# Attention masks written straight from comparisons, their assembly moved to ACT and GpSimd, and the parameters loaded from ACT's queue

## The chip, the cores and the metric

The kernel runs on one core of a Trainium2 chip. The metric is the device time of one execution in microseconds (us), lower being better; the median of a few executions is compared. Engines are named as in the profile: PE (TensorE matmul), PEld (its weight loads), DVE (VectorE), ACT (ScalarE), POOL (GpSimd) and SP (SyncE, which issues most of the DMAs here).

## What is computed

Sliding-window attention with a few sink columns, then two feed-forward layers on the 1536 tokens that come out of it.

```
B, H, S, D = 2, 8, 768, 64;  n_sink, window = 4, 128        # both arrive at run time
scores = q @ k.T / sqrt(D)
keep   = (pos_k < n_sink) | ((0 <= pos_q - pos_k) & (pos_q - pos_k < window))
a      = softmax(where(keep, scores, -1e9));  x = a @ v     # 1536 x 512
x = (h * clip(h + 3, 0, 6) / 6) @ w_out    with h = x @ w_in      # d_ff = 2048
y = (h * sigmoid(1.702 * h)) @ w_out2      with h = x @ w_in2     # d_ff = 2048
```

## The kernel before

**Tiles.** The tokens are taken in 12 tiles of 128 queries, T0 to T11, six to each batch. A query tile sees its own keys, those of the tile ahead and the four sinks: 196 columns, put side by side in an order of their own. Three mask tiles of 128x196 hold 0 where a score is kept and LOW = -1e9/SCALE where it isn't: `masks[0]` for the first tile of a batch, `masks[1]` for the second, `masks[2]` for all others.

**One tile's softmax.** A tile is done in two halves ("duos") of two head pairs. For each duo PE makes the scores (L743, 48 matmuls in the trace). For each of its four heads DVE adds the mask and finds the row's extreme in one instruction (L758), ACT takes the exponential (L766), and DVE and ACT scale by the inverse sum (L774, L775, L783, L785). PE transposes (L794), ACT or DVE copies the result out of PSUM (`pts`), and PE multiplies by the values (L817, L825). ACT and DVE then write the tile's x as two parts, `xyh` and `xyl` (L844). The feed-forward layers follow with L509 (up) and L577 (down), every product in three parts; their weights arrive packed in `stage` and DVE and ACT unpack and split them (L421 to L449, L405, L490).

**Who sets the order.** The part ahead of the fast path (constants, parameters, masks) is ordered by the tile framework's scheduler. From `fast_path` on, `Plan` records every operation with the engines that could do it and a cost on each, and its `issue` places them one after another by those costs. The result is a fixed order for each engine, and each engine works through its own in order. PSUM has eight banks, given out by the plan.

**The start.** SP loads `par_i` (window and n_sink as integers, spread over 128 partitions), then the keys and queries of T0 and T1 (`wf` from `in_kq`; later kq tiles use the same names), their values (`vb`, `vc`), the first weights (`stage`), and so on; eight of SP's loads can be under way, and each further one waits until the load eight places ahead has landed. DVE makes `flag` out of `par_i` (all parameters within what the fast path can do), every engine loads that flag and branches on it (L187), and behind the branch stands the fast path. Between flag and branch DVE makes the window and sink numbers (`par`, L194 to L201) and the masks' parts: `cur` (this tile's own keys), `prv` (the keys of the tile ahead), `snk` and `nos` (the sinks kept, and the sinks dropped since the ordinary columns hold them). Each part is made as ones and zeros and then turned into 0 and LOW by a second instruction (L230). `masks[0]` is put together there (L233, L234). Behind the branch the plan's first operations make `prv1` (L677) and copy the twelve pieces of `masks[1]` and `masks[2]` (L403 on ACT, L405 on DVE and POOL), on whichever engine its costs favour.

Of the kernel before, what the change touches and what calls it, by code (L numbers as in the profile page):

```python
# [9 lines left out]
F32 = mybir.dt.float32  # L10
F32R = mybir.dt.float32r
BF16 = mybir.dt.bfloat16
I32 = mybir.dt.int32
AF = mybir.ActivationFunctionType
ALU = mybir.AluOpType
PSUM = bass.MemoryType.PSUM

P = 128
SINKS = 4
HALF = 64  # L20
BIG = 1.0e9
# [42 lines left out]
def tile_sink_window_attention_moe_moe2(  # L64
# [10 lines left out]
    nc = tc.nc  # L75
# [7 lines left out]
    SCALE = 1.0 / math.sqrt(D)  # L83
# [16 lines left out]


    par_i = const.tile([P, 4], I32, name="par_i")
    nc.sync.dma_start(out=par_i, in_=params.bitcast(I32).unsqueeze(0).to_broadcast([P, 4]))

    tok = [(b, i) for b in range(B) for i in range(NI)]
    NTILE = len(tok)
# [45 lines left out]
    for kind, n in FIRST:  # L152
# [30 lines left out]
        out=ge, in0=ge, in1=le, scale=1.0, scalar=0.0, op0=ALU.mult, op1=ALU.add, accum_out=okay  # L183
# [5 lines left out]
    lo_f = const.tile([P, 2], F32, name="lo_f")  # L189
    hi_f = const.tile([P, 2], F32, name="hi_f")  # L190
    neg = const.tile([P, 2], F32, name="neg")
    par = const.tile([P, 2], F32, name="par")
    par_v = par_i.rearrange("p (a b) -> p b a", b=2)
    nc.vector.tensor_copy(lo_f, par_v[:, 0, :])  # L194
    nc.vector.tensor_copy(hi_f, par_v[:, 1, :])

    nc.vector.tensor_scalar(
        out=neg, in0=lo_f, scalar1=0.0, scalar2=2.0**32, op0=ALU.is_lt, op1=ALU.mult
    )
    nc.vector.tensor_tensor(out=lo_f, in0=lo_f, in1=neg, op=ALU.add)  # L200
    nc.vector.scalar_tensor_tensor(  # L201
        out=par, in0=hi_f, scalar=2.0**32, in1=lo_f, op0=ALU.mult, op1=ALU.add
    )
    win = par[:, 0:1]
    nsk = par[:, 1:2]

# [4 lines left out]
    cur = const.tile([P, P], F32, name="cur")  # L211
    prv = const.tile([P, P], F32, name="prv")
    prv1 = const.tile([P, HALF], F32, name="prv1")
    snk = const.tile([P, HALF], F32, name="snk")
    nos = const.tile([P, HALF], F32, name="nos")
    LOW = -BIG / SCALE
    with tc.tile_pool(name="msk", bufs=1) as mp:
        grid = mp.tile([P, P], F32, name="grid")
        nc.gpsimd.iota(grid, pattern=[[-1, P]], base=0, channel_multiplier=1, allow_small_or_imprecise_dtypes=True)
        colc = mp.tile([P, HALF], F32, name="colc")  # L220
        nc.gpsimd.iota(colc, pattern=[[1, HALF]], base=0, channel_multiplier=0, allow_small_or_imprecise_dtypes=True)
        t0 = mp.tile([P, P], F32, name="t0")
        nc.gpsimd.memset(masks[0], LOW)
        nc.vector.tensor_scalar(out=t0, in0=grid, scalar1=0.0, scalar2=None, op0=ALU.is_ge)
        nc.vector.scalar_tensor_tensor(out=cur, in0=grid, scalar=win, in1=t0, op0=ALU.is_lt, op1=ALU.mult)
        nc.vector.tensor_scalar(out=snk, in0=colc, scalar1=nsk, scalar2=None, op0=ALU.is_lt)
        nc.vector.tensor_scalar(out=nos, in0=colc, scalar1=nsk, scalar2=None, op0=ALU.is_ge)
        nc.vector.tensor_scalar(out=prv, in0=grid, scalar1=float(P), scalar2=win, op0=ALU.add, op1=ALU.is_lt)
        for m in (cur, snk, prv, nos):
            nc.vector.tensor_scalar(  # L230
                out=m, in0=m, scalar1=1.0, scalar2=BIG / SCALE, op0=ALU.subtract, op1=ALU.mult
            )
        nc.vector.tensor_tensor(out=masks[0][:, HALF:P], in0=cur[:, :HALF], in1=snk, op=ALU.max)  # L233
        nc.vector.tensor_copy(masks[0][HALF:, P : P + HALF], cur[HALF:, HALF:])  # L234

# [163 lines left out]
    def copy(eng, out, in_):  # L401
        if eng is nc.scalar:
            eng.copy(out, in_)  # L403
        else:
            eng.tensor_copy(out, in_)  # L405
# [257 lines left out]
    def plan_attention(plan, pool, due):  # L663
# [5 lines left out]
        for t in pexps:  # L669
# [2 lines left out]
        top, low = slice(0, HALF), slice(HALF, P)  # L672
        both = slice(0, P)
        mask_b = [Buf() for _ in masks]
        prv_b = Buf()
        plan.op(
            [("DVE", 150)], lambda e: e.tensor_tensor(out=prv1, in0=prv[:, :HALF], in1=nos, op=ALU.min), None,  # L677
            writes=[prv_b],
        )
        parts = []  # L680
        for m, first in ((1, prv1), (2, prv)):
            parts += [
# [3 lines left out]
            ]  # L686
        for m, rows, a, n, src, x in parts:
            plan.op(
                [("ACT", 190), ("DVE", 110), ("POOL", 300)],
                lambda e, m=m, rows=rows, a=a, n=n, src=src, x=x: copy(  # L690
                    e, masks[m][rows, a : a + n], src[rows, x : x + n]
                ),
                None, reads=[prv_b], adds=[mask_b[m]],
            )

        kq_b = [Buf(kqt[T], at=landed.get(("kq", T))) for T in range(EARLY + KEPT)]
# [164 lines left out]
    def fast_path():  # L861
        with tc.manual_schedule(), tc.tile_pool(name="mlp", bufs=1) as pool, tc.tile_pool(
# [34 lines left out]
            def item_due(items):  # L897
# [4 lines left out]
                return due  # L902

            plan_attention(plan, ap, pair_due)
            plan_mlps(plan, BLOCKS, item_due)
            plan.issue()
# [160 lines left out]
```

## Time and profile before

| | |
|---|---|
| median of 3 executions | 634.97 us (634.57 to 635.03) |
| profiled execution, its own time | 633.52 us |
| span of the profile (first to last instruction) | 631.6 us |
| around the span | 1.9 us |
| busy: PE, PEld, DVE, ACT, POOL | 609.3, 495.3, 503.7, 260.3, 2.4 us |
| mean granted TensorE clock | 0.996 |

The page splits the span into 40 slices. PE is busy in nine tenths or more of nearly all of them; only the first two or three (some 16 us each) are not full. DMA is busy for all of the first 30 us and much less behind that. The profiled execution was 1.45 us shorter than the median of the three runs.

### The profile page before, as it was taken

How to read it: one execution, taken by the hardware profiler on the slowest of the kernel's cores; microseconds unless marked ns; L12 is line 12 of the kernel's file. 1: busy time of each engine (PE TensorE's matmuls, PEld its weight loads, DVE VectorE, ACT ScalarE, POOL GpSimd, SP SyncE). 2: the span in 40 equal slices, each digit the busy share in tenths (PEclk: the TensorE clock that was granted, in tenths of full speed). 3: DMA queues.
4: the chain of work that ended last, by engine and by line, in shares of the span. 5: the costliest groups of instructions: out<-in, count | busy, mean ns of one | idle time of the engine just before them, and what ended most of it. 6: DMA issues, size and time to landing. Idle time of an engine off the chain costs nothing.

```text
span 631.6 us, 10569 instructions
## 1 busy us (share of the span) xinstructions
PE 609.3 (96%) x4224; PEld 495.3 (78%) x4224; DVE 503.7 (80%) x1065; ACT 260.3 (41%) x548; POOL 2.4 (0%) x19
## 2 busy tenths in 40 slices
PE   4789999999999999999999999999999999999996
PEld 4667878887788888888888888888888888888885
DVE  7799999999857587699999999865766666766752
ACT  5887787766537221164443644212311112211111
POOL 1000000000000000000000000000000000000000
PEclk9999999999999999999999999999999999999999
DMA  8974442563400000003443323000100000100001
GB/s 265 377 220 139 158 160 85 172 205 134 155 1 2 1 1 0 1 7 137 153 171 116 129 90 133 1 0 1 67 2 0 1 1 1 67 0 1 0 1 71
DMA packets 11175, 50.91 MB, mean 81 GB/s; under 512 B 1456, under 2 KB 1456, under 8 KB 7024
## 3 DMA queue, kind: packets, MB, share of 16 engines
q1 hardware_dynamic: 11120, 50.18, 23.5%
q8 instruction: 35, 0.57, 0.4%
q14 instruction: 20, 0.16, 0.1%
HBM read 47.02 MB, written 3.15 MB: 79 GB/s over the span
## 4 chain that ended last, share of the span: by engine, by line
PE 79%; DVE 12%; ACT 4%; DMA 3%; issue 1%; SPq 0%; ACTq 0%; DVEq 0%
PE bank L509 37%; PE bank L577 37%; PE bank L743 2%; DMA stage<-in_w_dram 2%; DVE wf L449 2%; DVE pexp L758 2%; DVE wf L442 1%; ACT pexp L766 1%; PE bank L794 1%; DVE u L526 1%; DVE w1l L490 1%; DVE w0l L490 1%; PE bank L817 1%; DVE wf L434 1%; PE bank L825 1%
## 5 line engine op out<-in xcount | busy, mean ns | idle before, releaser
L509 PE MATMUL bank<-xyh,w0h 128*128 128x512 f32 x384 | 154.3, 402 | 1.4 <-ACT pts L403 0.7
L509 PE MATMUL bank<-xyl,w0h 128*128 128x512 f32 x384 | 151.1, 393 | 1.1 <-DVE xyl L844 1.1
L509 PE MATMUL bank<-xyh,w0l 128*128 128x512 f32 x384 | 151.6, 395 | 0.0
L535 ACT ACTIVATE u<-bank 128x512 f32<-128x512 f32 x48 | 28.8, 599 | 179.7 <-PE bank L509 179.6
L509 PEld LDWEIGHTS bank<-xyh,w0h 128*128 128x128 f32 x384 | 72.1, 188 | 18.4 <-ACT pts L403 0.9
L509 PEld LDWEIGHTS bank<-xyh,w0l 128*128 128x128 f32 x384 | 72.0, 187 | 18.0 <-DVE w0l L490 0.2
L509 PEld LDWEIGHTS bank<-xyl,w0h 128*128 128x128 f32 x384 | 72.1, 188 | 17.1 <-DVE xyl L844 1.4
L577 PE MATMUL bank<-gh,w1h 128*128 128x512 f32 x192 | 77.1, 402 | 0.0
L577 PE MATMUL bank<-w1h,gh 128*128 128x512 f32 x192 | 75.9, 395 | 0.0
L577 PE MATMUL bank<-gh,w1l 128*128 128x512 f32 x192 | 75.3, 392 | 0.6 <-DVE w1l L490 0.6
L577 PE MATMUL bank<-w1l,gh 128*128 128x512 f32 x192 | 75.4, 392 | 0.0
L577 PE MATMUL bank<-gl,w1h 128*128 128x512 f32 x192 | 75.1, 391 | 0.0
L577 PE MATMUL bank<-w1h,gl 128*128 128x512 f32 x192 | 75.1, 391 | 0.0
L405 DVE CAST w0h<-wf 128x512 fp32r<-128x512 f32 x81 | 34.4, 424 | 50.0 <-PE bank L509 49.9
L490 DVE TENSOR_TENSOR w0l<-wf,w0h 128x512 fp32r<-128x512 f32 x96 | 66.1, 689 | 4.8
L552 DVE TENSOR_TENSOR gl<-u,gh 128x512 fp32r<-128x512 f32 x96 | 66.1, 689 | 1.9
L490 DVE TENSOR_TENSOR w1l<-wf,w1h 128x512 fp32r<-128x512 f32 x96 | 66.1, 689 | 1.2
L521 ACT ACTIVATE u<-bank,three 128x512 f32<-128x512 f32 x48 | 33.0, 687 | 79.5 <-PE bank L509 79.2
L405 DVE CAST w1h<-wf 128x512 fp32r<-128x512 f32 x61 | 26.0, 427 | 35.9 <-PE bank L577 35.4
L766 ACT ACTIVATE pexp<-pexp,nb 128x196 f32<-128x196 f32 x96 | 43.2, 452 | 11.0 <-DVE nb L758 10.9
L577 PEld LDWEIGHTS bank<-w1h,gl 128*128 128x128 f32 x192 | 36.1, 188 | 8.6
L577 PEld LDWEIGHTS bank<-gh,w1l 128*128 128x128 f32 x192 | 36.1, 188 | 8.5 <-DVE w1l L490 0.9
(96 smaller groups left out, 819.0 us busy)
## 6 DMA issues: line engine op xcount, KB each, us to landing
stage<-in_w_dram SPq DMA_DIRECT2D x32, 1024.0 KB, 4.9
wf<-in_kq_dram SPq DMA_DIRECT2D x8, 520.0 KB, 11.1
vc<-in_vc_dram SPq DMA_DIRECT2D x12, 320.0 KB, 4.0
out_dram<-u SPq DMA_DIRECT2D x12, 256.0 KB, 2.1
vb<-in_v_dram SPq DMA_DIRECT2D x10, 256.0 KB, 6.1
kq<-in_kq_dram SPq DMA_DIRECT2D x4, 520.0 KB, 10.9
vb<-in_v_dram SPq DMA_DIRECT2D x4, 128.0 KB, 6.4
par_i<-in_params_dram SPq DMA_DIRECT2D x1, 2.0 KB, 2.8
```

Source lines behind the costliest of these rows:

```text
L405: eng.tensor_copy(out, in_)
L434: lambda e: e.tensor_scalar(out=w.tile, in0=w.tile, scalar1=3, scalar2=0x3FFFFFF8, op0=ALU.logical_shift_left, op1=ALU.bitwise_and,),
L449: lambda e: e.scalar_tensor_tensor(out=w.tile, in0=low, scalar=29, in1=w.tile, op0=ALU.logical_shift_right, op1=ALU.bitwise_or),
L490: lambda e: e.tensor_tensor(out=lo.tile, in0=src.tile.bitcast(F32)[:, cols], in1=hi.tile.bitcast(F32), op=ALU.subtract),
L509: e.matmul(h.tile[:, :n], w, x, start=(c == 0 and k == 0), stop=(c == NC - 1 and k == 2))
L521: lambda e: e.activation(u.tile[:, :n], h.tile[:, :n], AF.Relu, bias=three, scale=1.0),
L535: lambda e: e.activation(u.tile[:, :n], h.tile[:, :n], AF.Sigmoid, scale=1.702),
L552: lambda e: e.tensor_tensor(out=gl.tile[:, :n], in0=u.tile[:, :n], in1=gh.tile[:, :n].bitcast(F32), op=ALU.subtract),
L577: e.matmul(yb.tile, l, r, start=(begin and k == 0), stop=(end is not None and k == 2))
L743: e.matmul(sc[j].tile[c * HALF : (c + 1) * HALF, o : o + n], here[r, q0 + c * HALF : q0 + (c + 1) * HALF], src[r, at : at + n], start=True ...
L758: lambda e, j=j, n=n, cols=cols: e.tensor_tensor_reduce(out=pes[n].tile[:, :W], in0=sc[j].tile[:, cols], in1=masks[kind], scale=-SCALE, sc ...
L766: lambda e, n=n: e.activation(pes[n].tile[:, :W], pes[n].tile[:, :W], AF.Exp, bias=nbs[n].tile, scale=-1.0, accum_out=z.tile[:, n : n + 1],),
```

## The change

The parameters' load goes from SP's queue to ACT's. The parts of the masks come out of one comparison each: a comparison for "dropped" gives 1, and the second operation of the same instruction multiplies by LOW (`cur` still needs a second instruction). The distance to the tile ahead's keys has an iota of its own, `far`. `masks[0]`'s parts are written first, and `prv1` moves ahead of the branch. Behind the branch all six copies for `masks[1]` are given to ACT and all six for `masks[2]` to POOL; DVE has none.

```diff
-    nc.sync.dma_start(out=par_i, in_=params.bitcast(I32).unsqueeze(0).to_broadcast([P, 4]))
+    nc.scalar.dma_start(out=par_i, in_=params.bitcast(I32).unsqueeze(0).to_broadcast([P, 4]))
...
+        far = mp.tile([P, P], F32, name="far")
+        nc.gpsimd.iota(far, pattern=[[-1, P]], base=P, channel_multiplier=1, allow_small_or_imprecise_dtypes=True)
...
-        nc.vector.tensor_scalar(out=t0, in0=grid, scalar1=0.0, scalar2=None, op0=ALU.is_ge)
-        nc.vector.scalar_tensor_tensor(out=cur, in0=grid, scalar=win, in1=t0, op0=ALU.is_lt, op1=ALU.mult)
-        nc.vector.tensor_scalar(out=snk, in0=colc, scalar1=nsk, scalar2=None, op0=ALU.is_lt)
-        nc.vector.tensor_scalar(out=nos, in0=colc, scalar1=nsk, scalar2=None, op0=ALU.is_ge)
-        nc.vector.tensor_scalar(out=prv, in0=grid, scalar1=float(P), scalar2=win, op0=ALU.add, op1=ALU.is_lt)
-        for m in (cur, snk, prv, nos):
-            nc.vector.tensor_scalar(
-                out=m, in0=m, scalar1=1.0, scalar2=BIG / SCALE, op0=ALU.subtract, op1=ALU.mult
-            )
+        nc.vector.tensor_scalar(out=t0, in0=grid, scalar1=0.0, scalar2=None, op0=ALU.is_lt)
+        window_of_params()
+        nc.vector.scalar_tensor_tensor(out=cur, in0=grid, scalar=win, in1=t0, op0=ALU.is_ge, op1=ALU.max)
+        nc.vector.tensor_scalar(out=snk, in0=colc, scalar1=nsk, scalar2=LOW, op0=ALU.is_ge, op1=ALU.mult)
+        nc.vector.tensor_scalar(out=cur, in0=cur, scalar1=LOW, scalar2=None, op0=ALU.mult)
         nc.vector.tensor_tensor(out=masks[0][:, HALF:P], in0=cur[:, :HALF], in1=snk, op=ALU.max)
         nc.vector.tensor_copy(masks[0][HALF:, P : P + HALF], cur[HALF:, HALF:])
+        nc.vector.tensor_scalar(out=prv, in0=far, scalar1=win, scalar2=LOW, op0=ALU.is_ge, op1=ALU.mult)
+        nc.vector.tensor_scalar(out=nos, in0=colc, scalar1=nsk, scalar2=LOW, op0=ALU.is_lt, op1=ALU.mult)
+        nc.vector.tensor_tensor(out=prv1, in0=prv[:, :HALF], in1=nos, op=ALU.min)
...
-        plan.op(
-            [("DVE", 150)], lambda e: e.tensor_tensor(out=prv1, in0=prv[:, :HALF], in1=nos, op=ALU.min), None,
-            writes=[prv_b],
-        )
...
             plan.op(
-                [("ACT", 190), ("DVE", 110), ("POOL", 300)],
+                [("ACT", 190) if m == 1 else ("POOL", 300)],
```

`window_of_params` is the five instructions that make `par`, unchanged.

DVE first, from `par` to its first L758. The mask tiles' numbers are those of the program: mask_153 to mask_155 are `masks[0]` to `masks[2]` before and mask_148 to mask_150 after; prv_158 before and prv_153 after are `prv1`. The first 12 rows before, behind L200:

```order
L201 SCALAR_TENSOR_TENSOR par<-hi_f,lo_f 128x2
L224 TENSOR_SCALAR t_168<-grid 128x128
L228 TENSOR_SCALAR prv<-grid,par 128x128
L225 SCALAR_TENSOR_TENSOR cur<-grid,par,t_168 128x128
L230 TENSOR_SCALAR prv<-prv 128x128
L226 TENSOR_SCALAR snk<-colc,par 128x64
L227 TENSOR_SCALAR nos<-colc,par 128x64
L230 TENSOR_SCALAR cur<-cur 128x128
L230 TENSOR_SCALAR snk<-snk 128x64
L230 TENSOR_SCALAR nos<-nos 128x64
L234 COPY mask_153<-cur 64x64
L233 TENSOR_TENSOR mask_153<-cur,snk 128x64
```

Then, before, the branch and behind it `prv1` and seven copies, ahead of the first L758:

```order
L187 TENSOR_LOAD flag
L998 COMPARE_AND_BRANCH
L677 TENSOR_TENSOR prv_158<-prv,nos 128x64
L405 COPY mask_154<-prv 128x64
L405 COPY mask_154<-snk 64x4
L405 COPY mask_154<-cur 64x64
L405 COPY mask_155<-prv 128x64
L405 COPY mask_155<-cur 128x64
L405 COPY mask_155<-cur 64x64
L405 COPY mask_155<-snk 64x4
L758 ISA pexp,nb<-bank,mask_153 128x196
```

After, from `t` (behind `par`, now L202) to the first L758, which is L756 in the changed file:

```order
L228 TENSOR_SCALAR t_165<-grid 128x128
L230 SCALAR_TENSOR_TENSOR cur<-grid,par,t_165 128x128
L232 TENSOR_SCALAR cur<-cur 128x128
L235 TENSOR_SCALAR prv<-far,par 128x128
L231 TENSOR_SCALAR snk<-colc,par 128x64
L234 COPY mask_148<-cur 64x64
L236 TENSOR_SCALAR nos<-colc,par 128x64
L233 TENSOR_TENSOR mask_148<-cur,snk 128x64
L237 TENSOR_TENSOR prv_153<-prv,nos 128x64
L187 TENSOR_LOAD flag
L996 COMPARE_AND_BRANCH
L756 ISA pexp,nb<-bank,mask_148 128x196
```

DVE has nine instructions instead of eleven from `t` to the branch, though one of them, `prv1`, used to stand behind it; between the branch and the first L758 it has none instead of eight.

ACT, from its first row to the first exponential (L766 before, L764 after); before:

```order
L1062 UNCONDITIONAL_BRANCH
L167 ACT_TABLE_LOAD
L167 ACTIVATE warm<-three 128x1
L187 TENSOR_LOAD flag
L998 COMPARE_AND_BRANCH
L403 COPY mask_154<-cur 128x64
L403 COPY mask_154<-snk 64x4
L403 COPY mask_155<-snk 64x4
L766 ACTIVATE pexp,z<-pexp,nb 128x196 x8
```

And after:

```order
L103 DMA par_i<-in_params_dram 128x4
L167 ACT_TABLE_LOAD
L167 ACTIVATE warm<-three 128x1
L187 TENSOR_LOAD flag
L996 COMPARE_AND_BRANCH
L406 COPY mask_149<-prv 128x64
L406 COPY mask_149<-cur 128x64
L406 COPY mask_149<-snk 64x4
L406 COPY mask_149<-prv_153 64x64
L406 COPY mask_149<-cur 64x64
L406 COPY mask_149<-snk 64x4
L764 ACTIVATE pexp,z<-pexp,nb 128x196 x8
```

ACT issues the parameters' load ahead of all its work and has six copies instead of three ahead of its first exponential, the last three of them behind one that reads `prv1`. POOL has six copies behind its branch instead of two. SP's rows are the same without its first load. PE's rows, and those of DVE and ACT from the first L758 and the first exponential on, stand in the same order as before.

## Rows read from the trace of the kernel before

**Rows 1.** The page's first part: busy us of each engine.

```profile
PE 609.3 (96%) x4224; PEld 495.3 (78%) x4224; DVE 503.7 (80%) x1065; ACT 260.3 (41%) x548; POOL 2.4 (0%) x19
```

**Rows 2.** Timeline of PE: start, us; in brackets idle before and its releaser.

```profile
5.40 2.88 PE L743 MATMUL bank<-wf 64*64 64x64 f32 x96 [5.40 <-DMA wf<-in_kq_dram]
...
14.50 0.44 PE L817 MATMUL bank<-pts,vb 128*64 128x128 f32 x4
...
17.88 0.34 PE L743 MATMUL bank<-wf,wf 64*64 64x64 f32 x8 [1.34 <-DVE pexp L785]
21.56 0.28 PE L743 MATMUL bank<-wf 64*64 64x64 f32 x3 [1.00 <-issue]
27.83 0.28 PE L743 MATMUL bank<-wf 64*64 64x64 f32 x4 [1.66 <-issue]
...
35.09 0.22 PE L743 MATMUL bank<-wf 64*64 64x68 f32 x1 [1.46 <-issue]
```

**Rows 3.** Stretches: length; busy us (count) of each engine; clock, DMA share, GB/s.

```profile
15.00:21.50 6.50, 4.21 (x132) 3.73 (x129) 5.22 (x26) 6.50 (x23) 0.00 (x0) 1.00 1.04 334
...
21.50:27.82 6.32, 4.62 (x127) 4.10 (x126) 5.36 (x21) 5.27 (x18) 0.00 (x0) 1.00 1.02 405
27.82:35.08 7.26, 5.63 (x126) 4.85 (x127) 5.85 (x29) 5.74 (x20) 0.00 (x0) 0.76 0.89 283
...
40.00:50.00 10.00, 8.56 (x122) 7.05 (x122) 9.93 (x33) 9.02 (x27) 0.00 (x0) 1.00 0.62 185
```

**Rows 4.** DMA queues in 18.90 to 20.15: packets, MB, share.

```profile
q8 instruction: 1, 0.02, 5.4%
```

**Rows 5.** Timeline of SP: start, us it took to issue.

```profile
0.73 0.40 SPq L103 DMA_DIRECT2D par_i<-in_params_dram  x1
1.19 0.88 SPq L121 DMA_DIRECT2D wf<-in_kq_dram  x2
...
5.43 0.48 SPq L121 DMA_DIRECT2D wf<-in_kq_dram  x1
```

**Rows 6.** DMA issues at 0.73, 1.19, 5.43 alone: KB, us to landing.

```profile
par_i<-in_params_dram SPq DMA_DIRECT2D x1, 2.0 KB, 2.8
...
wf<-in_kq_dram SPq DMA_DIRECT2D x1, 520.0 KB, 4.1
...
wf<-in_kq_dram SPq DMA_DIRECT2D x1, 520.0 KB, 12.3
```

**Rows 7.** Timeline of DVE from `par` to the first L758.

```profile
4.38 0.16 DVE L201 SCALAR_TENSOR_TENSOR par<-hi_f,lo_f 128x2 f32<-128x2 f32 x1
4.46 0.22 DVE L224 TENSOR_SCALAR t<-grid 128x128 f32<-128x128 f32 x1
...
5.05 0.72 DVE L230 TENSOR_SCALAR prv<-prv 128x128 f32<-128x128 f32 x1
...
5.72 0.23 DVE L227 TENSOR_SCALAR nos<-colc,par 128x64 f32<-128x64 f32 x1
5.88 0.21 DVE L230 TENSOR_SCALAR cur<-cur 128x128 f32<-128x128 f32 x1
...
6.55 0.23 DVE L233 TENSOR_TENSOR mask<-cur,snk 128x64 f32<-128x64 f32 x1
7.06 0.23 DVE L677 TENSOR_TENSOR prv<-prv,nos 128x64 f32<-128x64 f32 x1 [0.29 <-DVE mask L233]
...
8.35 0.36 DVE L758 CUSTOM_DVE_ANT_0 pexp<-bank,mask 128x196 f32<-128x196 f32 x1
```

**Rows 8.** Timeline of POOL behind its branch.

```profile
4.95 0.73 POOL L670 MEMSET pexp<- 128x60 f32 x8 [3.17 <-DVE prv L228]
7.35 0.43 POOL L405 COPY mask<-prv 64x64 f32<-64x64 f32 x2 [1.67 <-DVE prv L677]
```

**Rows 9.** Timeline of ACT around its first exponential.

```profile
6.45 0.41 ACT L403 COPY mask<-snk 64x4 f32<-64x4 f32 x2
8.75 0.46 ACT L766 ACTIVATE pexp<-pexp,nb 128x196 f32<-128x196 f32 x1 [1.89 <-DVE nb L758]
```

More of the change, by code (lines that the diff above doesn't have):

```diff
@@ L192, in tile_sink_window_attention_moe_moe2, with window_of_params @@
     par = const.tile([P, 2], F32, name="par")
-    par_v = par_i.rearrange("p (a b) -> p b a", b=2)
-    nc.vector.tensor_copy(lo_f, par_v[:, 0, :])
-    nc.vector.tensor_copy(hi_f, par_v[:, 1, :])
-    nc.vector.tensor_scalar(
-        out=neg, in0=lo_f, scalar1=0.0, scalar2=2.0**32, op0=ALU.is_lt, op1=ALU.mult
-    )
-    nc.vector.tensor_tensor(out=lo_f, in0=lo_f, in1=neg, op=ALU.add)
-    nc.vector.scalar_tensor_tensor(
-        out=par, in0=hi_f, scalar=2.0**32, in1=lo_f, op0=ALU.mult, op1=ALU.add
-    )
+    def window_of_params():
+        par_v = par_i.rearrange("p (a b) -> p b a", b=2)
+        nc.vector.tensor_copy(lo_f, par_v[:, 0, :])
+        nc.vector.tensor_copy(hi_f, par_v[:, 1, :])
+        nc.vector.tensor_scalar(
+            out=neg, in0=lo_f, scalar1=0.0, scalar2=2.0**32, op0=ALU.is_lt, op1=ALU.mult
+        )
+        nc.vector.tensor_tensor(out=lo_f, in0=lo_f, in1=neg, op=ALU.add)
+        nc.vector.scalar_tensor_tensor(
+            out=par, in0=hi_f, scalar=2.0**32, in1=lo_f, op0=ALU.mult, op1=ALU.add
+        )
     win = par[:, 0:1]
@@ L223, in tile_sink_window_attention_moe_moe2 @@
         nc.gpsimd.memset(masks[0], LOW)
-        nc.vector.tensor_scalar(out=t0, in0=grid, scalar1=0.0, scalar2=None, op0=ALU.is_ge)
-        nc.vector.scalar_tensor_tensor(out=cur, in0=grid, scalar=win, in1=t0, op0=ALU.is_lt, op1=ALU.mult)
-        nc.vector.tensor_scalar(out=snk, in0=colc, scalar1=nsk, scalar2=None, op0=ALU.is_lt)
-        nc.vector.tensor_scalar(out=nos, in0=colc, scalar1=nsk, scalar2=None, op0=ALU.is_ge)
-        nc.vector.tensor_scalar(out=prv, in0=grid, scalar1=float(P), scalar2=win, op0=ALU.add, op1=ALU.is_lt)
-        for m in (cur, snk, prv, nos):
-            nc.vector.tensor_scalar(
-                out=m, in0=m, scalar1=1.0, scalar2=BIG / SCALE, op0=ALU.subtract, op1=ALU.mult
-            )
+        nc.vector.tensor_scalar(out=t0, in0=grid, scalar1=0.0, scalar2=None, op0=ALU.is_lt)
[3 more added lines that the diff above has]
+        nc.vector.tensor_scalar(out=cur, in0=cur, scalar1=LOW, scalar2=None, op0=ALU.mult)
         nc.vector.tensor_tensor(out=masks[0][:, HALF:P], in0=cur[:, :HALF], in1=snk, op=ALU.max)
         nc.vector.tensor_copy(masks[0][HALF:, P : P + HALF], cur[HALF:, HALF:])
+        nc.vector.tensor_scalar(out=prv, in0=far, scalar1=win, scalar2=LOW, op0=ALU.is_ge, op1=ALU.mult)
+        nc.vector.tensor_scalar(out=nos, in0=colc, scalar1=nsk, scalar2=LOW, op0=ALU.is_lt, op1=ALU.mult)
+        nc.vector.tensor_tensor(out=prv1, in0=prv[:, :HALF], in1=nos, op=ALU.min)
     ENG = {"PE": nc.tensor, "ACT": nc.scalar, "DVE": nc.vector, "POOL": nc.gpsimd, "SP": nc.sync}
@@ L674, in plan_attention @@
         mask_b = [Buf() for _ in masks]
-        prv_b = Buf()
-        plan.op(
-            [("DVE", 150)], lambda e: e.tensor_tensor(out=prv1, in0=prv[:, :HALF], in1=nos, op=ALU.min), None,
-            writes=[prv_b],
-        )
         parts = []
@@ L692, in plan_attention @@
                 ),
-                None, reads=[prv_b], adds=[mask_b[m]],
+                None, adds=[mask_b[m]],
             )
```

## The prediction

> **What bounds the kernel now.** The busy shares come first: PE 96% of the span, DVE 80%, the others far less [rows 1]. The change touches nothing of the long feed-forward part, so the question is what ends PE's waits in the first 40 us, where PE isn't full, and whether what the change moves is ahead of those waits. I therefore went next to PE's timeline, looking only at rows with idle time in brackets [rows 2]. The reader should see two kinds of wait there.
>
> Two are for keys. PE starts at 5.40; the first kq load was issued at 1.19 and took 4.1, so it landed at 5.3 [rows 2, 5, 6]. T2's scores start at 17.88; the profile puts this wait down to DVE's L785, but the kq load issued at 5.43 took 12.3 and landed at 17.7, again 0.1 to 0.2 ahead of PE [rows 2, 5, 6]. So the DMA was in any case due there. That load took three times as long as the first because the queue ahead of it was full: the DMA share is 1.04 in the stretch 15.0 to 21.5 [rows 3].
>
> The other three, of 1.00, 1.66 and 1.46 us, end at 21.56, 27.83 and 35.09 and have the releaser "issue": PE waited for nothing that the profile shows. All end in the middle of a duo's scores, where no operand is new. Between the first and the second PE and PEld have 127 + 126 instructions, between the second and the third 126 + 127 [rows 3]: equal pieces of 253 records. In 18.90 to 20.15, ahead of the first, a single packet of 0.02 MB travels on a queue of the kind "instruction" [rows 4]. I read these waits as PE waiting for its next piece of code. The pieces then follow one another in 6.3 and 7.3 us, though PE had work for only 4.6 and 5.6 of them [rows 3]. Counting back, 15.0 to 21.5 holds 132 + 129 records, so the piece ahead of 21.56 was entered at about 15.1. This is within T0's values, which start at 14.50 [rows 2]. If entering a piece is what sends for the next, T0's values set the pace of everything up to 35.09, and T0's values hang on the softmax of T0, which starts with L758 at 8.35 [rows 7].
>
> The Trainium skill ("Runtime: NRT & Kernel Launch", Instruction fetch mechanics) says that an engine's code comes in blocks of 256 instructions, each fetched by DMA while the one ahead of it runs, and that this is mostly hidden. The trace agrees on the size within lost records, and not on the hiding, with 4.1 us of waits. By the page's "hidden", T2's keys alone would be the gate, and the sum below would be 0.46 whatever the parameters' load does.
>
> Behind 35.09 PE makes T2's values, and DVE is busy 9.93 of 10 us from 40 to 50 [rows 3], in a fixed order. A shift at 35.09 is then passed on, since no load there has a time of its own (each waits for a buffer).
>
> **The change, part by part.**
>
> *DVE ahead of its first L758.* The parameters land at 0.73 + 2.8 = 3.5, `par` is made at 4.38, `t` ends at 4.68 [rows 5 to 7]. The second instruction on `cur` now needs `cur`, which needs `t`; I put it at 5.05, where the second one on `prv` stood. That one took 0.72 where its twin on `cur` took 0.21 [rows 7]; POOL's memsets run from 4.95 to 5.68 [rows 8], and I let the new one end with them as well, at 5.77. Before, six instructions from there (5.72) to the end of `masks[0]` took 6.78 - 5.72 = 1.06 [rows 7]. Now five are left (`prv` ends beside the stalled one): 5/6 of 1.06 is 0.88, so 6.65. The branch costs the same 0.29 [rows 7] and the first L758 follows directly: 6.93, which is 1.42 earlier than 8.35. The other bound comes from POOL: its copies take 0.43 / 2 = 0.21 each [rows 8] and six of them now run beside these five DVE instructions. If four of the five wait for a copy each, that is 0.85 more: 7.8, or 0.57 earlier. I take 7.25, **1.1 earlier**, nearer to the first, since nothing but the memsets shows such a wait.
>
> *ACT.* Its copies take 0.41 / 2 = 0.2 each [rows 9]. The last three wait for `prv1`, ready at 7.25 - 0.29 = 6.96, and end at about 7.6. The first exponential follows L758 by 8.75 - 8.35 = 0.40 [rows 7, 9], that is at 7.65. So the copies are just covered; without that cover they would cost up to 0.2. Each of the eight exponentials then comes as early as the first.
>
> *POOL.* `masks[2]` is needed at T2's first L758, behind 17.4. Six copies of 0.2 from about 6 on are hidden by ten us.
>
> *The parameters' load.* ACT can issue it at the same 0.73, but SP's first kq load now goes out beside it and no longer 0.46 behind it [rows 5]. How late the 2 KB become is not shown before. Lower bound nothing: they arrive 2.8 after issue. Upper bound: they land together with the 520 KB that they travel beside, 4.1 - 2.8 = 1.3 later [rows 6]. I take the middle, **0.65 late**. All of DVE's masks, the flag and every engine's branch stand behind it.
>
> *SP's loads.* All go out 0.46 earlier, the kq load for T2 included, so its scores can start at 17.4. PE would then reach the end of its piece at 21.56 - 1.00 - 0.46 = 20.1, ahead of the code; this gain is hidden by the wait for code. If that wait were gone, 0.46 and up to 1.00 more would show.
>
> *PE's start.* POOL's first instruction behind the branch stands at 4.95 [rows 8], so PE can start at about 5.0 plus the delay, 5.65 instead of 5.40. T0's first duo is half of 2.88 [rows 2], so its scores end at 7.1. L758 at 7.25 + 0.65 = 7.9 doesn't wait for them.
>
> **Sum:** 1.1 - 0.65 = **0.45 us** earlier at T0's values, and by the pieces of code at 35.09 and at the end. The profiled execution would go from 631.6 + 1.9 = 633.5 to 633.1; on the median of the runs, which stands 1.45 above it, **634.5 us**. The bounds: 0.57 - 1.3 gives 0.73 later, 635.7. At the other end 1.42 with no delay is capped, because the piece entered at 15.1 was itself sent for when PE began T0's last scores (about 8.2); PE would start 0.35 earlier, and the piece takes 6.3 or more, so it is there at 14.2. That caps the gain at 0.9 to 1.2: 633.8.
>
> **The rivals.**
>
> 1. *Keys, not code, are the gate at T2.* Then PE follows SP's loads: 0.46, 634.5, whatever the delay. For it: 17.7 against 17.88. Against it: PE waits again at 21.56 with all its keys there.
> 2. *No delay, and the code comes with less waiting:* PE is bound by T2's keys and its own work, 0.46 + 1.00 = 1.46 earlier, 633.5. For it: par_i's packets are tiny. Against it: the cap above.
> 3. *Nothing arrives at the end:* the delay is near 1.1 and eats the gain, or DVE and the weights' loads behind 40 us take it back: 635.0.
> 4. *The parameters come late (slower).* A packet on a queue beside SP's can wait long: the code asked for at about 15.1 had its packet behind 18.9, 3.8 us [rows 3, 4]. If par_i waits 3.8, T0's L758 comes 2.7 later than before: 637.7. A delay over 1.1 makes a loss, one over 2.4 a loss of more than 0.2%. Against it: at 0.73 nothing is queued yet. The Trainium skill ("DMA: Bandwidth & Descriptors", Queues, rings and completion order) says that each DMA engine takes turns between queues packet by packet, which would put the small load between the first kq packets and not behind all of SP's; no run here shows it yet. The same page (Issuing engines are not separate DMA queues) says that a second issuing engine saves only the time of issue, 0.46 here.
>
> **How the numbers follow.** About 0.2%, 1.27 us, is what a measurement of this kernel can tell from no change. Chances: the forecast (net 0.2 to 0.9) 0.42; rival 1 0.15, rival 2 0.15, rival 3 0.18, rival 4 0.10. Only rival 2 is faster by more than 0.2% and only rival 4 slower. The range reaches from just above rival 2 to the bound of the sum, 633.6 to 635.7; it leaves out rival 4 and half of rival 2.
>
> **What would show each step.** DVE's first L758 near 7.9 (7.25 plus the delay); par_i landing between 3.5 and 4.8; no copy on DVE between branch and L758; T0's values starting about 0.45 earlier; waits "issue" in the same three places of the scores, ending each by that much earlier, 253 records apart; T2's scores at about 17.4. The prediction is wrong if par_i lands past 5, if the three waits shrink or keep their old times while T0's values move, or if DVE's masks are slowed by POOL past 7.8.

## The result and the profile after

The changed kernel takes 638.23 us (median of 4 executions, 637.17 to 638.82) against 634.77 (633.75 to 635.03) of the kernel before run beside it: a ratio of 1.0056 [1.0037, 1.0074], 3.46 us slower. The forecast was 634.5, within 633.6 to 635.7. What came is rival 4, the late parameters, though not by the way that it gave.

The profiled execution took 637.17 us with a span of 635.5: 3.65 and 3.9 more than before. The busy times tell nothing of it. The page's first part after the change (compare [rows 1]):

```profile
PE 608.8 (96%) x4224; PEld 494.9 (78%) x4224; DVE 502.1 (79%) x1055; ACT 261.2 (41%) x551; POOL 3.3 (1%) x24
```

PE, PEld and DVE are each a little less busy. So the loss is waiting, and the start is where to look. DMA issues at 0.73 in the changed kernel: KB, us to landing (compare [rows 6]):

```profile
wf<-in_kq_dram SPq DMA_DIRECT2D x1, 520.0 KB, 5.3
par_i<-in_params_dram ACTq DMA_DIRECT2D x1, 2.0 KB, 5.4
```

Both go out at 0.73. The parameters now take 5.4 us instead of 2.8, and the first key load beside them 5.3 instead of 4.1. DVE of the changed kernel, from its first work on the parameters to its first mask addition (compare [rows 7]):

```profile
6.27 0.16 DVE L180 TENSOR_TENSOR ge<-par_i,least 128x4 f32<-128x4 int32 x1 [5.21 <-DMA par_i<-in_params_dram]
...
7.75 0.67 DVE L232 TENSOR_SCALAR cur<-cur 128x128 f32<-128x128 f32 x1
...
9.27 0.21 DVE L237 TENSOR_TENSOR prv<-prv,nos 128x64 f32<-128x64 f32 x1
10.05 0.36 DVE L756 CUSTOM_DVE_ANT_0 pexp<-bank,mask 128x196 f32<-128x196 f32 x1 [0.57 <-PE bank L741]
```

Before, the parameters landed at 3.5 and the first mask addition stood at 8.35, 4.85 behind. Now it stands at 10.05, 3.9 behind 6.17: the masks are made about one us faster, and 2.66 us too late. PE of the changed kernel, rows with idle time and T0's first values (compare [rows 2]):

```profile
7.79 2.89 PE L741 MATMUL bank<-wf 64*64 64x64 f32 x96 [7.79 <-DVE cur L230]
...
16.14 0.44 PE L815 MATMUL bank<-pts,vb 128*64 128x128 f32 x4
...
19.27 0.34 PE L741 MATMUL bank<-wf,wf 64*64 64x64 f32 x8 [1.09 <-DVE pexp L783]
...
23.54 0.28 PE L741 MATMUL bank<-wf 64*64 64x64 f32 x3 [1.59 <-issue]
...
29.81 0.28 PE L741 MATMUL bank<-wf 64*64 64x64 f32 x4 [1.66 <-issue]
...
37.17 0.22 PE L741 MATMUL bank<-wf 64*64 64x68 f32 x1 [2.62 <-issue]
```

T0's values come 1.64 later, T2's scores 1.39, and the three waits for code end 1.98, 1.98 and 2.08 later. They stand at the same places of the program.

The rest of the loss lies further on. Behind 37 the shift stays near 2.1 until a load of weights, 7.0 us under way instead of 6.4, holds ACT for 0.94, to 120.85; the same instruction before stood at 117.72 without a wait. Part of that is given back, and the last store is issued at 630.44 instead of 627.88, 2.56 later. The other 1.35 us lie behind that store: the span ends 5.03 us after it, where it ended 3.68 after it before. In that stretch a packet of code travels on another queue than the one whose packet came ahead of PE's wait (q8, [rows 4]). DMA queues in 633.2 to 633.4 of the changed kernel:

```profile
q14 instruction: 1, 0.01, 17.2%
```

So there were three things to explain: why the parameters come late, why the late start is passed on in full, and what the 1.35 us at the end are.

### The profile page after: what moved, and what is told of

Read it like the earlier page. It is cut to its first block, busy times and chain, and to the rows that moved or that the text cites. A ratio compares the mean times of both kernels' runs of the same rounds, so it can differ in the third digit from the quotient of the medians.

```text
span 635.5 us, 10565 instructions
## 1 busy us (share of the span) xinstructions
PE 608.8 (96%) x4224; PEld 494.9 (78%) x4224; DVE 502.1 (79%) x1055; ACT 261.2 (41%) x551; POOL 3.3 (1%) x24
## 4 chain that ended last, share of the span: by engine, by line
PE 78%; DVE 12%; ACT 4%; DMA 2%; issue 2%; DVEq 0%; ACTq 0%
PE bank L512 37%; PE bank L580 37%; DMA stage<-in_w_dram 2%; DVE pexp L756 2%; PE bank L741 1%; DVE wf L452 1%; ACT pexp L764 1%; DVE wf L445 1%; PE bank L792 1%; DVE u L529 1%; DVE w1l L493 1%; DVE w0l L493 1%; PE bank L815 1%; DVE wf L429 1%; DVE pexp L783 1%
## 5 line engine op out<-in xcount | busy, mean ns | idle before, releaser
L764 ACT ACTIVATE pexp<-pexp,nb 128x196 f32<-128x196 f32 x96 | 43.2, 453 | 9.9 <-DVE nb L756 9.8
L424 ACT ACTIVATE wf<-stage 128x1024 f32<-128x1024 f32 x32 | 36.9, 1153 | 16.6 <-DMA stage<-in_w_dram 14.6
```

The source lines that it names most:

```text
L424: lambda e: e.activation(w.tile.bitcast(F32), top.bitcast(F32), AF.Abs),
L764: lambda e, n=n: e.activation(pes[n].tile[:, :W], pes[n].tile[:, :W], AF.Exp, bias=nbs[n].tile, scale=-1.0, accum_out=z.tile[:, n : n + 1],),
```

## The experiments

Unless said otherwise the start of a run is read in its profile, and its median stands beside that of the kernel before in the same series (634.83, 634.63 and 634.95 in the three series).

**1. The changed kernel with the parameters back on SP's queue.**

```diff
-    nc.scalar.dma_start(out=par_i, ...)
+    nc.sync.dma_start(out=par_i, ...)
```

> The changed kernel with the parameters' load back at the head of SP's queue; masks and copies stay changed. Theory A (the small load takes turns with the key loads that start beside it, and DVE's masks, the flag and all branches wait for it): the parameters land at 3.5 again instead of 6.2, the first mask addition on DVE stands at about 7.4 instead of 10.05, T0's values come about 1 us earlier than in the kernel before, PE's three waits for nothing shown end near 20.6, 26.9 and 34.1, and the time is about 633.8, or 635.1 if ACT's wait of 1.3 us in the closing barrier stays. Theory B (the masks' new order, with POOL's six copies beside DVE, costs the time): little changes, about 637 to 638.

Measured: 634.87 on 634.83, ratio 1.0 [0.9985, 1.0016]. The loss is gone: without the load on ACT's queue it doesn't come. The parameters land at 3.45 and the first mask addition stands at 7.34. But T0's values, 1.06 earlier, bring nothing further on. PE of this run:

```profile
13.44 0.44 PE L815 MATMUL bank<-pts,vb 128*64 128x128 f32 x4
...
17.44 0.34 PE L741 MATMUL bank<-wf,wf 64*64 64x64 f32 x8 [1.97 <-SPq L1060]
21.44 0.38 PE L741 MATMUL bank<-wf 64*64 64x64 f32 x3 [0.25 <-issue]
...
27.72 0.28 PE L741 MATMUL bank<-wf 64*64 64x64 f32 x4 [1.40 <-issue]
```

T2's keys land at 17.31, so PE idles 1.97 there. Behind that wait the granted clock fell, here in the windows 17.4 to 21.0 and 21.0 to 27.7 (columns as in [rows 3]; the third number from the end is the clock):

```profile
17.40:21.00 3.60, 3.56 (x90) 3.19 (x91) 3.04 (x12) 3.34 (x9) 0.00 (x0) 0.68 1.03 360
21.00:27.70 6.70, 5.07 (x129) 4.31 (x126) 5.16 (x21) 4.92 (x17) 0.00 (x0) 0.91 1.01 402
```

Full speed, 2.4 GHz, is 1.00 and the lower level, 1.2 GHz, 0.50: a mean of 0.68 is about two thirds of the window at the lower one ((1 - 0.68) / 0.5). PE reached the border of its piece only just ahead of the code. The wait's length alone doesn't tell when the clock falls: in 17.4 to 21.0 of experiment 8 it stayed at 1.00 behind a wait of 1.86 at the same place.

**2. The kernel before with the parameters on ACT's queue, and nothing else.** The same line, the other way.

> The kernel before with one line changed: the parameters' load goes out from ACT's queue. Theory A: they land at about 6.2, the first mask addition comes at about 11.0 instead of 8.35, the three waits of PE end about 2.7 later, and the time is 637 to 638. Theory B: only the key loads move, 0.46 earlier, and the time is 634.3 to 634.8.

Measured: 636.87 on 634.83, 1.003 [1.0016, 1.0045]. The load alone loses 2.0 us. It lands at 5.36, T0's values start at 16.34 and the first wait for code ends at 23.65, 2.1 later than before. The end behind the last store is 3.60: the third part of the loss is not the load's.

**3. A second small load of the parameters at the head of SP's queue.**

```diff
     nc.scalar.dma_start(out=par_i, ...)
+    par_x = const.tile([P, 4], I32, name="par_x")
+    nc.sync.dma_start(out=par_x, ...)
```

> The changed kernel with a second small load of the parameters (into a tile that nothing reads) at the head of SP's queue, so that SP's key loads go out 0.46 later, as in the kernel before, while the one that counts stays on ACT's queue. Theory A: with this head start ACT's load lands at 3.5 to 4.2, and the first mask addition at 7.4 to 8.1. A rival (a load from ACT's queue is slow in itself): it lands at about 6 again and the time stays at 637 to 638.

Measured: 638.79, 1.0066 [1.0041, 1.009]. The head start over the keys didn't help. DMA issues from 0.73 to 1.22 of this run:

```profile
wf<-in_kq_dram SPq DMA_DIRECT2D x1, 520.0 KB, 7.5
par_i<-in_params_dram ACTq DMA_DIRECT2D x1, 2.0 KB, 6.2
par_x<-in_params_dram SPq DMA_DIRECT2D x1, 2.0 KB, 5.9
```

Even the copy that stood first in SP's queue took 5.9 instead of 2.8. So it is not the size of the keys' packets by which the small load is late. Either ACT's queue is slow, or it is enough that two queues work at once.

**4. The kernel before with four tiny activations more on ACT.**

```diff
+    nc.scalar.activation(warm, three, AF.Exp)     # four times
```

> The kernel before with four more tiny activations on ACT in its idle time at 2.2 us, which is as many instructions as the change adds to ACT. Theory A (1.3 us of the loss is a wait for code on ACT in the closing barrier, which comes up because ACT's program got four instructions longer): the start keeps its times, and the stretch from the last issue of an output to the end of the span grows from 3.7 to about 5.0 us, so the time is about 636. Rival (the long closing stretch in the profile of the changed kernel was an accident of that execution): no change, 634.8.

Measured: 634.94, 1.0007 [0.9989, 1.0026]. The profile shows the third part alone: start and waits as before (first mask addition 8.34, waits ending at 21.51, 27.79, 34.95), the last store issued at 627.97, and 4.75 us from there to the end of a span of 632.72 instead of 3.68. The timed runs scatter by more than this one us and don't resolve it.

**5. The first seven loads from ACT's queue.** SP issues the others; the parameters stay at the head of ACT's.

> The changed kernel with the first seven loads of keys, values and weights issued from ACT's queue too, behind the parameters' load, so that no second queue works beside it. Theory B (turns): each DMA engine takes the two queues' packets in turn, and a packet of 16 bytes takes about as long a turn as one of 4 KB, so the 144 packets of par_i and the first 128 of the first key load come out together; with one queue only, par_i's come first again, and it lands near 3.5 (2.8 us after issue), the first L756 stands near 7.4. Rival (ACT's queue is slow in itself): par_i still lands past 5, and the first L756 stands past 9.

Measured: 635.75 (one execution). It told nothing apart: SP's next two loads went out at 0.73 and 1.21 all the same, so two queues did work at once, and the parameters took 4.7. Experiment 9 mends this.

**6. Sixteen score products of T1 made twice, in PE's idle time.**

```diff
+    for again in range(2 if d == 3 and x < 2 else 1):
         e.matmul(sc[j].tile[...], ..., start=True, stop=True)
```

> The kernel before with 16 matmuls of T1's second duo done twice (same operands, same place, in PE's idle time between 9.5 and 11.5), that is 32 more PE instructions ahead of T0's transposes and no other change. Theory C (the code pieces set the pace and are counted in instructions): the next piece is entered in T0's second transposes near 14 instead of in T0's values at 15.2, and sends for its follower about 1 us earlier; the waits marked issue come 32 records earlier in the program and end about 1 us earlier (20.5, 26.8, 34.1), and the time falls by up to 1 us: 633.8 on 634.8. Rival (T0's values, or T2's keys, set the pace): T0's values at 14.5 as before, the waits end at 21.6, 27.8, 35.1 or later by the 16 matmuls (0.5 us), and the time is 634.8 to 635.3.

Measured: 635.01 on 634.63, 1.0002 [0.9988, 1.0016]. Each product is two matmuls with their loads, so 64 instructions were added, not 32. PE of this run:

```profile
13.81 0.49 PE L744 MATMUL bank<-wf 64*64 64x68 f32 x2 [2.64 <-issue]
17.48 0.44 PE L818 MATMUL bank<-pts,vb 128*64 128x128 f32 x4
...
23.13 0.28 PE L744 MATMUL bank<-wf,wf 64*64 64x64 f32 x3 [1.34 <-issue]
...
29.45 0.33 PE L818 MATMUL bank<-pts,vb 128*64 128x128 f32 x2 [2.35 <-issue]
```

A new wait of 2.64 stands in T1's scores, where PE never stopped before, and the border that stood in scores at 27.83 now falls into values. So the borders are counted in instructions: this part of the theory holds. The other part, that an earlier entry sends earlier for the next piece by as much, fails: the piece entered at 13.81 was followed by the next only at 23.13, 9.3 us later, where it had been 6.6 (from 14.95, 256 instructions ahead of 21.56, to there).

**7. The comparisons alone:** parameters on SP, copies on the engines of the plan's choice.

> The comparisons alone: the changed kernel with the parameters' load on SP's queue and the plan's own choice of engine for the twelve copies, as before the change. If the shorter masks give most of DVE's gain, the first L756 stands near 7.5 to 7.8 (before: 8.35; with the copies moved too: 7.34); if the copies give it, near 8.2.

Measured: 635.73 (one execution); the first mask addition stands at 8.31, against 8.35 before and 7.34 with the copies moved too. DVE of this run:

```profile
6.53 0.22 DVE L237 TENSOR_TENSOR prv<-prv,nos 128x64 f32<-128x64 f32 x1
7.25 0.20 DVE L408 COPY mask<-prv 128x64 f32<-128x64 f32 x1 [0.50 <-issue]
...
8.31 0.36 DVE L756 CUSTOM_DVE_ANT_0 pexp<-bank,mask 128x196 f32<-128x196 f32 x1
```

`prv1` stands ahead of the branch now, 0.53 earlier than in [rows 7], but the branch costs 0.50 instead of 0.29, the first copy starts at 7.25 where it started at 7.21, and six copies follow instead of seven. DVE's gain is the copies' leaving.

**8. Experiment 1 with three of `masks[1]`'s six copies on POOL,** so that ACT's program is as long as before.

```diff
-                [("ACT", 190) if m == 1 else ("POOL", 300)],
+                [("ACT", 190) if at < 3 else ("POOL", 300)],
```

> The changed kernel with the parameters' load on SP's queue and with three of the six copies of masks[1] on POOL instead of ACT, so that ACT's program is as long as before. Theory D (ACT's last instructions stand in a piece of code that comes late): from the last load or store issue to the end of the span 3.7 us instead of 4.8 to 5.0, so about 1.1 us less than with all six on ACT: 633.8 on 634.9. Rival (the long end has another cause, or is hidden in the timed runs): 4.8 again, or 634.9.

Measured: 634.1 on 634.63, 0.999 [0.9971, 1.001]. From the last store to the end 4.12 us, where experiment 1 had 4.77. The waits for code (0.77, 1.66 and 1.53) end at 20.88, 27.16 and 34.42, 0.7 earlier than before: here two thirds of T0's 0.96 came through. The medians can't tell 0.5 us from nothing.

**9. All first loads from ACT's queue.** ACT is held until 10 by its issues; only the start is read.

> The changed kernel with all of the first loads, the parameters' first, on ACT's queue, so that SP's queue is empty until the fast path (in the run with seven of them there SP's next two loads went out at 0.73 and 1.21 after all, beside the parameters). ACT is held up by its issues, so only the start is to be read. Theory B (two queues in turns): par_i lands near 3.5, 2.8 us after issue, and DVE's first work on it stands near 3.6. Rival (ACT's queue is slow in itself): par_i lands past 5.

Measured: 635.23 (one execution). DMA issues from 0.73 to 1.22 of this run:

```profile
wf<-in_kq_dram ACTq DMA_DIRECT2D x1, 520.0 KB, 4.1
par_i<-in_params_dram ACTq DMA_DIRECT2D x1, 2.0 KB, 2.8
```

DVE's first work on the parameters, with its wait for them:

```profile
3.62 0.16 DVE L184 TENSOR_TENSOR ge<-par_i,least 128x4 f32<-128x4 int32 x1 [2.56 <-DMA par_i<-in_params_dram]
```

ACT's queue alone is as quick as SP's, 2.8 and 4.1. What makes the load late is that a second queue works beside it.

**10. The changed kernel with ACT's program shortened as in 8.** The parameters stay on ACT's queue.

> The changed kernel with three of the six copies of masks[1] on POOL instead of ACT, and the parameters still on ACT's queue. Theory D (ACT's closing instructions stand behind a border of its code): ACT's program is then one instruction longer than before instead of four; from the last store's issue to the end 3.6 to 3.8 us instead of 5.03, and the start as late as in the changed kernel (first L756 near 10.0): 636.9, 1.3 less than the changed kernel's 638.2 and 2.1 above before. Rival (the long end isn't seen in the timed runs): 638.2.

Measured: 635.86 on 634.95, 1.0015 [1.0002, 1.0028]; less of a loss than expected. The end behind the last store is 4.0 us (issued at 628.49, span 632.5). The parameters landed at 5.33 in this profile, 0.84 ahead of the changed kernel's, and the waits for code end at 22.30, 28.58 and 36.21, 1.2, 1.2 and 1.0 ahead of it. It has the parameters as late as experiment 2 (5.36) with the masks changed: T0's values start at 15.36 instead of 16.34, so with a late load the masks' gain of 0.98 is passed on.

**11. Experiment 8 with T2's keys sent ahead of the first weights.** Nothing else moves on PE, DVE and ACT.

> The changed kernel with the parameters on SP's queue and three copies of masks[1] on POOL (634.1 on 634.6), and the first 1-MB load of weights sent behind T2's keys instead of ahead of the values of T1; the order on PE, DVE and ACT is the same. T2's keys land about 2.8 us earlier, near 14.5, so T2's scores follow T0's values near 16.3 and don't wait. Theory C (the code pieces are the gate): PE comes to the border of its piece at 18.5 to 19 and waits there until about 20.9, as it did; the later waits end at 27.2 and 34.4, and the time is the same, 634.1. Rival 1 of the prediction (keys are the gate): the waits end 1.9 us earlier and the time is near 632.3.

Measured: 635.34 on 634.95, 1.0014 [0.9998, 1.003]. The keys land at 14.26 instead of 17.3. PE of this run:

```profile
14.53 0.22 PE L825 MATMUL bank<-pts,vc 68*64 68x64 f32 x1 [0.39 <-issue]
...
21.73 0.28 PE L743 MATMUL bank<-wf 64*64 64x64 f32 x3 [3.00 <-issue]
...
28.00 0.28 PE L743 MATMUL bank<-wf 64*64 64x64 f32 x4 [1.66 <-issue]
```

The wait at T2's scores is gone, and its whole gain is idle time at the border, 3.00 instead of 0.77. Rival 1 falls: with the keys there, PE still waits for its code. The first two waits end 0.85 and 0.84 later than in experiment 8, not at the same times as expected, so the code itself came later with the loads in this order.

**12. The kernel before with eight products made twice,** 32 instructions more.

> The kernel before with eight of T1's scores made twice, which is 32 PE instructions more (the run with sixteen had 64 more, since each of these products is two matmuls with their loads). The borders of PE's pieces stand at its 449th, 705th, 961st and 1217th instruction whatever these are. Theory C: the first border falls in T0's second transposes, near 14.0, where its code is just there; no new wait in T1's scores; T0's values at 14.5 to 14.9; the second border comes 32 instructions earlier in the program and its wait ends at 20.5 to 21.6. If a border's code took its time from T0's values instead, the waits would stay where they were in the program.

Measured: 634.53 (one execution). No new wait in T1's scores and T0's values at 14.65, as expected. The waits end at 21.62, 27.99 and 33.73, the second of them in values, so the borders moved again with the count. The first of them ends as late as before though the piece ahead of it was entered at 14.06 instead of 14.95.

## Why the prediction was wrong

**The step that failed** is the price of the parameters' load: "Lower bound nothing: they arrive 2.8 after issue. Upper bound: they land together with the 520 KB that they travel beside, 4.1 - 2.8 = 1.3 later". Of these bounds the prediction took the middle, 0.65; the load was 2.66 late. They did land together with the keys, 6.17 and 6.00. What was wrong is the 4.1, which is what the keys took with one queue at work. DMA queues from 1.7 to 4.0 (packets, MB, share of the engines), the kernel before first, then the changed kernel, then experiment 3:

```profile
q1 hardware_dynamic: 221, 0.32, 63.2%
```

```profile
q1 hardware_dynamic: 92, 0.38, 67.0%
q10 hardware_dynamic: 77, 0.00, 1.6%
```

```profile
q1 hardware_dynamic: 111, 0.01, 3.0%
q10 hardware_dynamic: 57, 0.00, 1.1%
```

q1 is SP's queue and q10 ACT's. The parameters are 144 packets of a few bytes, the keys 128 of 4 KB (520 KB) and a few small ones. With two queues 169 and 168 packets passed in this time, with one queue 221, and the number doesn't follow the bytes: in experiment 3 nearly all 168 were tiny and the DMA engines stood almost idle, while in the changed kernel more than half were 4 KB. The other three runs with two queues have 167 or 168 (2, 5 and 10), and the others with one queue 219 to 224. So two things made the load late. Its 144 packets no longer went first but in turns with as many big ones, and with two queues at work about a quarter fewer packets passed. Even with the parameters ahead of them in one queue the keys landed at 5.3; on a queue of their own, and issued 0.46 earlier, they landed at 6.0. Why two queues pass fewer packets than one stays open.

The Trainium skill ("DMA: Bandwidth & Descriptors", Queues, rings and completion order) has the engine take turns between queues. The counts agree in that both queues advance at the same time, but not always one for one: 92 and 77 in the changed kernel, 52 and 115 in experiment 10, where ACT's queue began first (the parameters landed at 5.33 there). The prediction cited the page as a reason against a long delay, since the small load would come between the first key packets. It did, and was 2.66 us late. The count of packets, and that two queues were at work, were the things to look at, not the bytes.

**The threshold was right.** Rival 4 said that a delay above 1.1 is a loss. 2.66 less the 1.01 that the masks gain (experiment 1) is 1.65; T0's values came 1.64 later. Its mechanism was another, a packet that waits behind a full queue, and that its 637.7 lies near 638.23 is luck: it had L758 2.7 later and nothing at the end of the span, and the first mask addition came 1.7 later and the end 1.35.

**DVE's first mask addition,** 1.1 earlier but for the load: 1.01 in experiment 1. The stalled second instruction on `cur` stood at 5.04 and ran 0.67, put at 5.05 with an end at 5.77. `prv1` ended at 6.77, put at 6.65, but the branch cost 0.56 instead of 0.29, so that 7.34 came near the middle value, 7.25, by a wait that wasn't in the sum and not by POOL. (The profile puts this wait down to PE's scores. But in the changed kernel PE's first duo, half of 2.89 from 7.79, was over at about 9.3, ahead of the end of `prv1` at 9.48, and PE's own start at 7.79 instead of 5.65 held nothing up.)

**ACT, POOL.** As predicted: in the changed kernel ACT's last copy starts at 9.93 and takes 0.19, and the first exponential follows the mask addition by 0.40; POOL's copies are done before 9.8.

**SP's loads.** The first went out at 0.73 as predicted. T2's keys, forecast to go out 0.46 earlier than 5.43, went out at 6.56, and landed at 19.13, where the forecast had T2's scores start at 17.4. A load waits until the one eight places ahead has landed, and the parameters still count among the eight, on whichever queue they travel. SP's own waits in 0 to 20 of the changed kernel have a row that the kernel before lacks (us in total, times, longest):

```profile
SPq L137 <- DMA par_i<-in_params_dram: 1.4, 1, 1.4
```

The prediction left this wait out: the late parameters delay the loads too. With the parameters on SP (experiment 1) T2's keys landed at 17.31.

**The pieces of code.** Windows between the waits of the changed kernel, as in [rows 3]:

```profile
23.54:29.81 6.27, 4.62 (x127) 4.10 (x126) 5.04 (x17) 5.19 (x17) 0.00 (x0) 1.00 1.02 406
29.81:37.17 7.36, 4.14 (x127) 3.54 (x128) 6.32 (x30) 6.30 (x22) 0.00 (x0) 1.00 0.94 279
```

253 and 255 records, as before; experiments 6 and 12 show that the borders follow the count, and 11 that they and not the keys hold PE. From the first of these waits to the second all is as read: their ends lie 6.27 to 6.38 apart in the kernel before, the changed one and experiments 1, 2, 4, 6, 7, 8, 10, 11 and 12, so a shift at the first is passed on. The link ahead of it is the weak one. That an entry "is what sends for the next", so that a shift at T0's values is passed on, holds roughly for a late start (1.64 became 1.98, in experiment 2 1.84 became 2.09, in 10 0.86 became 0.74) and not for an early one (1.06 became 0.12 in experiment 1, 0.96 became 0.68 in 8). Waits that keep their times while T0's values move were one of the prediction's own signs of being wrong. So even with no delay the forecast gain wouldn't have come in full: experiment 1 has none that its median can tell. SP's queue up to the second packet of PE's code, in the kernel before (to 19.03), the changed one (to 21.02) and experiment 12 (to 19.21):

```profile
q1 hardware_dynamic: 1608, 5.07, 88.8%
```

```profile
q1 hardware_dynamic: 1476, 5.17, 88.4%
```

```profile
q1 hardware_dynamic: 1605, 5.05, 88.5%
```

Whether T0's values start at 13.4 or at 16.1, that packet comes when SP's queue has moved 5.0 to 5.2 MB: also in experiments 1 (5.00), 4 (5.08), 7 (5.20), 8 (5.05), 10 (5.08) and 3 (5.14). It was 5.37 in 11, where the loads' order differs, 5.47 in 2, 5.73 in 6, and 6.2 and 6.9 on both queues in 9 and 5, where T0's values came only at 18.7 and 20.1. So the loads may pace the code as well as PE's entry does, and the loads are what the change delayed. This is read from these runs and not tested by itself: no run took loads away, and experiments 2 and 6 fit badly. What holds the packet back stays open.

**Not seen at all: ACT's end.** The change gives ACT four instructions more. The end behind the last store is 3.6 to 4.2 us with none or one more (before and experiments 2, 6, 7, 8, 10, 11, 12) and 4.75 to 5.03 with three or four more (the changed kernel and 1, 3, 4). With the nine and sixteen more of experiments 5 and 9 it is short again, 3.73 and 3.94. So it isn't the instructions' own time. The two closing semaphore steps of DVE and of ACT in the changed kernel (ns shortest/median/longest; first and last start, us):

```profile
L1060 DVEq EVENT_SEMAPHORE  x2: 21/21/21, 633.6 to 635.4; - x2
L1060 ACTq EVENT_SEMAPHORE  x2: 17/17/17, 634.9 to 635.2; - x2
```

In the kernel before both engines make the first of them at 631.0. Now ACT makes it 1.3 behind DVE, with the packet of code of 633.3 ahead of it, and every engine's second step is behind that. In experiment 4, with four more as well, ACT makes it at 632.4 and DVE at 631.1. In experiment 1, with three more, that step is on time and the drain behind it, the next instruction, is late (its last start):

```profile
L1060 DVEq DRAIN  x2: 10/34/58, 627.2 to 632.7; - x2
L1060 ACTq DRAIN  x2: 81/108/135, 631.5 to 633.7; - x2
```

One instruction less, and the wait falls one instruction later: this is how a border of ACT's code would move, and with three or four more it lies in the closing steps, where the engines wait for one another. In the profile this is 1.35 of the 3.9 us.

**The sum.** Span: 2.56 at the last store and 1.35 behind it. Of the 2.56, 2.08 stood at 37.17; the rest, 0.5, came with the weights' load. In the medians, the load alone costs 2.0 (experiment 2), and the changed kernel without the long end 0.9 (experiment 10), with a load that came 0.84 earlier in its profile. From there to the changed kernel's 3.46 it is 2.5, of which the long end explains at most 1.35; the rest isn't shown. The medians don't resolve the long end by itself: experiments 1 and 4 have it too, and stand 0.0 and 0.1 above the kernel before.

## What to carry to other kernels

A small load isn't free because it has few bytes: count its packets. If it is wanted first, leave it at the head of the one queue that is used then; a second queue beside it didn't put it ahead here but in turns with the big loads, and slowed both. Ask too which later loads wait for it to land. A gain at the start of a kernel whose code comes in while its loads fill the DMA may be held up at the next border of code, so look where the waits marked "issue" stand before counting on it. And when a change adds a few instructions to an engine, look at the very end of the span too.

## What the runs showed of the hardware that was not expected

- Two queues at once: a load of 2 KB in 144 packets took 4.6 to 6.2 us beside another queue (five runs) and 2.7 to 2.8 alone, from ACT's queue as from SP's. From 1.7 to 4.0 us 167 to 169 packets passed in those five runs and 219 to 224 in the nine with one queue, whatever their size.
- PE's waits for code stand about 256 instructions apart (253 to 255 records), and moved with the count when 32 or 64 instructions were added ahead of them. Which useful instructions a border falls on can be shifted with work in idle time; no run gained by it.
- A wait in the closing steps of ACT's program, read as a border of its code, cost about one us in the profiles: 4.75 to 5.03 behind the last store instead of 3.6 to 4.2, and nine more instructions made it vanish.
- PE's clock fell to the lower level in experiment 1 behind a wait of 1.97, a mean of 0.68 over 17.4 to 21.0, but a wait of 1.86 in experiment 8 and one of 3.00 in experiment 11 left it at 1.00 in the stretch behind them.
